# A ring of 21 exponential tiles instead of 14, and another order inside the steps of seven matmul pairs

## The chip, the core and the metric

The kernel runs on one core of a Trainium2 chip. Its engines work in parallel, each through its own queue of instructions in order: TensorE (PE; the loading of its weights is shown as PEld), VectorE (DVE), ScalarE (ACT), GpSimd (POOL), and SyncE (SP), which issues the DMA transfers. They wait for one another through semaphores. The metric is the device time of one execution in microseconds.

## The reference

Attention with one shared key and value head and 32 query heads, a dense layer with Mish, a second dense layer, and a gated residual, on 2048 rows of 512:

```python
xn = _layernorm(x, axis=-1)
# attention: H = 32 heads of Dh = 16, one k and one v for all heads
q = (xn @ wq).reshape(B, S, H, Dh).transpose(0, 2, 1, 3)
k, v = xn @ wk, xn @ wv
p = softmax(einsum("bhqd,bkd->bhqk", q, k) * Dh ** -0.5)
s = einsum("bhqk,bkd->bhqd", p, v).transpose(0, 2, 1, 3).reshape(B, S, H * Dh) @ wo
# dense 512 -> 1792, Mish, dense 1792 -> 512
h = xn @ w1 + b1
g = silu((h * tanh(softplus(h))) @ w2)
return x + s * g
```

## The kernel before

**What a step is.** The 2048 query rows are cut in 4 chunks of 512, the heads in groups of four. A chunk and a group make one of NU = 32 units, and a unit has 16 steps, one for each of the 16 tiles of 128 keys: 512 steps in all. TensorE's 128 rows are used as two lanes of 64 rows, each of which runs its own matmul beside the other's. A step issues on them:

- four scores `e` (line 908), keys by queries. ScalarE turns each into a tile `pt` of exponentials (line 910);
- four matmuls `m` (line 928), the same scores the other way round for a later unit. VectorE takes the maximum of each into `mb` (line 932). From these come the rows that are subtracted before the exponential. Once per unit they are folded and turned (`c_rows`, lines 951 to 961) and moved by DMA;
- up to eight products `xps` of a dense layer (line 112), at three matmuls for each product of 128 (high and low parts). Every product is cut in two halves of 64 rows: one step does the upper halves of a piece, the next the lower halves of the same piece, in the same bank of PSUM;
- last the four `pv` matmuls (line 982) of the exponentials of two steps earlier, which take all 128 rows, and stand in the trace as eight.

**The dense work.** A group of products ends in one 512-wide result. A projection to q, a tile of the first dense layer or of the output layer has 12 products, so two pieces of six and four steps; most thirds of the second dense layer have 15, so pieces of eight and seven. At the end of a group its bank is read out: on ScalarE as `hb` (line 671, first layer), `qf` (611, q) or `y` (739, first third), on VectorE as a sum into `y` (745, and line 156 for the output layer). POOL then splits and multiplies what was read out.

**Banks.** Of the eight banks three are for `e`, three for `m`, one is for `pv` and one for `xps`. Ring `pt` has NPT = 14 tiles of exponentials; the 16 tiles of x first land in the same ring, those beyond its size in two other buffers (`load_x`).

**What sets the order.** Nothing reorders at run time; the program writes each queue out. `waves` (line 537) writes one step. It has a list for the dense lane `h` (`b` and the products `xs`) and one for the other lane (`a`). `em` (line 1339) fills them: the four scores and n of the four maxima go to the other lane in the order of the string EM, the remaining 4 - n maxima to the dense lane, where they are issued after the products. With six or seven products n is 3: the other lane has seven matmuls, the dense lane six or seven products and one m. `waves` takes one of the dense lane and one of the other by turns; such two are called a pair here. The last of the other lane is kept until the products are all issued. What was issued on the other lane when the last product was out is called `relay`: the first product of the next step, in the same bank, is made to wait for ScalarE's or VectorE's instruction of it, unless a group has ended. The lanes change sides from step to step.

The names of this text: T is the first matmul of a step; the first exponential is that of the step's first score; a pair's place is counted from T.

Of the kernel before, what the change touches and what calls it, by code (L numbers as in the profile page):

```python
# [42 lines left out]
HOLD = 1  # L43
STEP_US = 2.95
XMAX = 8
NPT = 14
EM = "MEMEMEME"
MLAG = 4
NHB = 4
NXR = 2  # L50
# [12 lines left out]
def m_need(v):  # L63

    return (34, 64)[v] if v < 2 else 32 * (v + 1)
# [53 lines left out]
def block_kernel(ctx: ExitStack, tc: tile.TileContext, x, wq, wk, wv, wo, w1, b1, w2, out):  # L119
    nc = tc.nc  # L120
# [92 lines left out]
    def load_x(c):  # L213
        for tt in range(4):
            tag, n = ("pt", NPT) if 4 * c + tt < NPT else (("y0", "sc")[tt % 2], 1)
            xin[c, tt] = sb.tile([P, D], F32, tag=tag, name=f"xin{c}_{tt}", bufs=n)
# [252 lines left out]

    held = [None]  # L470
    evacs = [0]
    cur = {"g": None, "ps": None, "n": 0, "chunk": [], "relay": None}

    def is_ready(g):
        return (all(i.tile is not None and i.ready <= step[0] for i in g.items)
# [7 lines left out]
    def begin():  # L483
        prepare()
        if qqueue and is_ready(qqueue[0]):
            g = qqueue.popleft()
        elif queue and is_ready(queue[0]):
            g = queue.popleft()
        else:
            n = next((n for n, g in enumerate(queue) if g.wo is None), None)  # L490
            if not n or not is_ready(queue[n]) or queue[n].m1 is None:
                return False
            g = queue[n]
            del queue[n]
        if g.start:
            g.start()
        if g.alloc:
            ps = g.alloc()
        else:
            ps = ps_x.tile([P, 512], F32, tag="x", name="xps")  # L500
        cur.update(g=g, n=0, ps=ps, chunk=[], relay=None)
        return True

    def finish():
        g = cur["g"]
        if cur["n"] < len(g.mms):
            return False
        for i in g.items:
            i.users -= 1
        cur["g"] = None  # L510
        evacs[0] += g.dve
        if lead:
            lead["post"](g, cur["ps"])
        else:
            g.post(cur["ps"])
            g.done = step[0]
        return True
# [14 lines left out]
    def chunk_size(n):  # L532
        return -(-n // -(-n // XMAX)) if n else 0

    def waves(h, em, new):

        if not cur["chunk"] and (not new or cur["g"] is None and not begin()):  # L540
            mms = []
        else:
            g = cur["g"]
            mms = cur["chunk"] or g.mms[cur["n"]:cur["n"] + chunk_size(len(g.mms) - cur["n"])]
        second = bool(cur["chunk"])
        k = len(mms)
        ms = em(k)
        a = deque(ms[1 - h])
        b = deque(ms[h])
        ps = cur["ps"]  # L550
        ends = second and cur["n"] + k == len(cur["g"].mms)
        xs = deque(mms)
        relay = None
        first = True
        done = False
        while a or b or xs:
            if xs:
                i = xs.popleft().half(ps, h)
                if first and cur["relay"] is not None:
                    tc.add_manual_dep(i.ins, cur["relay"].ins.name, mybir.DependencyInfo(  # L560
                        mybir.DependencyClass.Sync, mybir.DependencyReason.DATA), reason="other half of the bank")
                first = False
                if ends and cur["g"].dve and len(xs) == HOLD:
                    held[0] = []
                if not xs and ends:
                    cur["n"] += k
                    cur["chunk"] = []
                    finish()
                    done = True
                    for top in held[0] or ():  # L570
                        top()
                    held[0] = None
            elif b:
                b.popleft()()
            if len(a) > 1 or a and not xs:
                r = a.popleft()()
                if k and not xs and relay is None:
                    relay = r
        if k and not done:
            assert relay is not None  # L580
            cur["relay"] = relay
            if second:
                cur["n"] += k
                cur["chunk"] = []
            else:
                cur["chunk"] = mms
# [310 lines left out]
    def e_one(s, i):  # L897

        v, r = divmod(s, 16)
        if s < NS - LEAD:  # L900
            a, k, p = 1 - s % 2, r - r % 2 + i // 2, i % 2
        else:
            a, k, p = i % 2, r, i // 2
        q = qt_of[v]
        o = 64 * a
        ps, tag = (ps_m, "m") if NS - LEAD <= s and i in ((1, 3) if s < NS - 4 else (3,)) else (ps_e, "e")
        e = ps.tile([P, C], F32, tag=tag, name=f"e{s}_{i}")
        pe.matmul(e, ks[o:o + 64, P * k:P * (k + 1)], q[o:o + 64, p], start=True, stop=True)  # L908
        pt = sb.tile([P, C], F32, tag="pt", name=f"pt{s}_{i}", bufs=NPT)
        r = act.activation(pt, e, AF.Exp, scale=0.25)  # L910
        pt_of[16 * v + k, p, a] = pt
        return r
# [24 lines left out]
    def m_sides(h, n):  # L937

        ahead = m_next[h] - m_next[1 - h]
        lo = max((4 - MLAG - ahead + 1) // 2, 4 - (32 * NU - m_next[1 - h]))  # L940
        hi = min((4 + MLAG - ahead) // 2, 32 * NU - m_next[h])
        return max(min(n, hi), lo)
# [116 lines left out]
    def due(t):  # L1059
        step[0] = t  # L1060
        for k in sorted(k for k in timed if k <= t):
            for fn in timed.pop(k):
                fn()
# [84 lines left out]
    for c0, c1 in ((0, 1), (1, 2), (2, 3), (3, 4)):  # L1148
# [4 lines left out]
        for c in range(c0, c1):  # L1153
            xs, scs = [], []
# [65 lines left out]
    def best(eng):  # L1220
        found = None
        for k in plan[eng]:
            s = k.start(T[eng])
            if s is not None:
                rank = max(s, T[eng] + 0.1) + WAIT_US * k.prio
                if found is None or rank < found[2]:
                    found = (s, k, rank)
        return found
# [5 lines left out]
    while True:  # L1234
# [7 lines left out]
        b = best("PE")  # L1242
# [13 lines left out]
        s, e, k = min(opts, key=lambda o: o[0])  # L1256
# [34 lines left out]
        elif k == "J":  # L1291
            tag = next((g for g in ("wq", "ws", "wb") if (g == "wq" or s > 19.0) and arrived(g) and busy[0] + E0 < s + 0.5), None)
            n = ran[0]
# [16 lines left out]
    while left:  # L1310
        k = next(k for k in left if all(d.end is not None for d in k.deps))
# [20 lines left out]
    for s in range(NS + 2000):  # L1332
        inm = s < NS - LEAD
        if inm or cur["chunk"]:
            assert s < NS
            due(s)
            h = s % 2

            def em(k):
                n = m_sides(1 - h, k // 2) if inm else 0  # L1340
                x = deque(lambda i=i: e_one(s, i) for i in range(4))
                y = deque(lambda: m_one(1 - h) for _ in range(n))
                r = [[], []]
                for op in EM:
                    if op == "M" and y:
                        r[1 - h].append(y.popleft())
                    elif op == "E":
                        r[1 - h].append(x.popleft())
                r[h] = [lambda: m_one(h) for _ in range(4 - n if inm else 0)]
                return r  # L1350

            if s >= 2 and (s - 1) % 16 == 0 and s > 1:
                gap[0] += 1
            waves(h, em, inm)
            act_jobs(1 + (len(jobs) > 2))
            due(s + 0.5)
            pv_to(s - 2)
            last = s + 1
        elif s < NS:
            if s == last and (NS - s) % 2:  # L1360
                for k in range(4):
                    e_one(s, k)
                due(s)
                fill(4)
                act_jobs(1)
                pv_to(s - 2)
            elif (NS - s) % 2 == 0:
                for k in range(6):
                    e_one(s + k // 4, k % 4)
                due(s)  # L1370
                fill(4)
                act_jobs(1)
            else:
                for k in range(2, 4):
                    e_one(s, k)
                due(s)
                fill(4)
                act_jobs(2)
                pv_to(s - 1)
        else:  # L1380
            due(s)
            act_jobs(100)
            pv_to(NS - 1)
            due(s + 0.5)
            fill(16)
        step[0] = s
        if vdone[0] < 8 * NC and min(m_next) >= m_need(vdone[0]):
            r = c_rows(vdone[0])
            rowq.extend([r[0], lambda r=r: (r[1](), r[2](), r[3]())])
            vdone[0] += 1  # L1390
        if rowq and not evacs[0]:
            rowq.popleft()()
        evacs[0] = 0
        pump()
        if s > NS + 1 and not queue and cur["g"] is None and not timed and not jobs:
            break
# [1 line left out]

# [10 lines left out]
```

## Time and profile before

| | |
|---|---|
| runs, median (lowest to highest) | 1607.55 us (1606.56 to 1608.75) |
| profiled execution, span | 1607.2 us |
| TensorE busy, granted clock | 1590.6 us, 0.996 |
| VectorE, ScalarE, GpSimd busy | 1344.9, 1298.3, 625.4 us |
| start until the first full step | some 93 us |
| regular steps, until some 1530 us | 357 with six products, 60 with seven, 56 with eight |
| end, scores and dense work without maxima | some 77 us |

The span is that of the profiled execution from its first instruction to its last, and is the time against which sums are made. A line of the profile's groups gives engine, operation, tiles, shape and count, then the busy time and the mean of one in ns, then the idle time of the engine before them and who ended it. A line of the timeline gives start and length in us, engine, line and tiles; "x4" are four instructions in a row, and square brackets hold the idle time before them and who ended it. In a table of stretches, each line has the stretch, its length, and for each engine the busy time and the number of instructions, then TensorE's clock and the DMA share.

### The profile page before, as it was taken

How to read it: one execution, taken by the hardware profiler on the slowest of the kernel's cores; microseconds unless marked ns; L12 is line 12 of the kernel's file. 1: busy time of each engine (PE TensorE's matmuls, PEld its weight loads, DVE VectorE, ACT ScalarE, POOL GpSimd, SP SyncE). 2: the span in 40 equal slices, each digit the busy share in tenths (PEclk: the TensorE clock that was granted, in tenths of full speed). 3: DMA queues.
4: the chain of work that ended last, by engine and by line, in shares of the span. 5: the costliest groups of instructions: out<-in, count | busy, mean ns of one | idle time of the engine just before them, and what ended most of it. 6: DMA issues, size and time to landing. Idle time of an engine off the chain costs nothing.

```text
span 1607.2 us, 31497 instructions
## 1 busy us (share of the span) xinstructions
PE 1590.6 (99%) x11611; PEld 847.8 (53%) x11611; DVE 1344.9 (84%) x2299; ACT 1298.3 (81%) x2512; POOL 625.4 (39%) x640
## 2 busy tenths in 40 slices
PE   9999999999999999999999999999999999999998
PEld 5445555555555555555555555555555555555544
DVE  8898888888888888888898988888888888888812
ACT  7478788688898778978988787787798878779885
POOL 3276278066355103612514322172152323315522
PEclk9899999999999999999999999999999999999999
DMA  6233133142321304212103231221331223022020
GB/s 192 72 116 96 51 108 115 29 149 83 101 90 38 111 16 140 64 48 88 39 24 109 64 116 44 87 71 35 96 109 58 83 61 97 24 96 70 8 86 27
DMA packets 73001, 125.08 MB, mean 78 GB/s; under 512 B 21520, under 2 KB 33808, under 8 KB 72848
## 3 DMA queue, kind: packets, MB, share of 16 engines
q1 hardware_dynamic: 72848, 123.08, 24.4%
q8 instruction: 92, 1.51, 0.4%
q14 instruction: 61, 0.50, 0.1%
HBM read 75.57 MB, written 26.21 MB: 63 GB/s over the span
## 4 chain that ended last, share of the span: by engine, by line
PE 96%; DVE 1%; ACT 1%; POOL 0%; DMA 0%; SPq 0%; issue 0%; DVEq 0%; POOLq 0%
PE xps L112 43%; PE pv L982 32%; PE e L908 9%; PE m L928 8%; PE xps L108 3%; PE kp L312 1%; DVE mb L932 1%; PE wop L108 1%; ACT pt L910 0%; PE xp L280 0%; DMA xin<-in_dram 0%; DVE xt L156 0%; SPq L217 0%; ACT hb L671 0%; PE ol L1045 0%
## 5 line engine op out<-in xcount | busy, mean ns | idle before, releaser
L932 DVE TENSOR_REDUCE mb<-m 128x1 f32<-128x512 f32 x2048 | 1271.2, 682 | 184.2 <-PE m L928 149.0
L910 ACT ACTIVATE pt<-e 128x512 f32<-128x512 f32 x2048 | 1068.2, 605 | 250.9 <-PE e L908 240.9
L928 PE MATMUL m<-ks,qt 48*128 48x512 f32 (+1 forms) x2048 | 845.8, 424 | 4.2 <-DVE mb L932 2.9
L908 PE MATMUL e<-qt,ks 64*128 64x512 f32 x2048 | 746.7, 408 | 2.4 <-ACT pt L910 1.6
L982 PE MATMUL pv<-pt,vaug 128*32 128x512 f32 x4096 | 543.1, 604 | 0.0
L928 PEld LDWEIGHTS m<-ks,qt 48*128 48x128 f32 (+1 forms) x2048 | 373.1, 186 | 76.3 <-DVE mb L932 38.0
L908 PEld LDWEIGHTS e<-qt,ks 64*128 64x128 f32 x2048 | 372.4, 186 | 26.2 <-ACT pt L910 11.1
L112 PE MATMUL xps<-xt,ws 64*128 64x512 f32 x1266 | 351.2, 409 | 0.9 <-ACT pt L910 0.4
L112 PEld LDWEIGHTS xps<-xt,ws 64*128 64x128 f32 x1266 | 218.0, 185 | 204.8 <-ACT pt L910 137.7
L112 PE MATMUL xps<-wbs,act 64*128 64x512 f32 x1188 | 321.3, 407 | 0.0
L112 PEld LDWEIGHTS xps<-wbs,act 64*128 64x128 f32 x1188 | 207.0, 185 | 168.7 <-ACT pt L910 103.9
L166 POOL TENSOR_SCALAR t<-t 128x512 f32<-128x512 f32 x56 | 34.4, 614 | 323.8 <-ACT t L679 323.8
L982 PEld LDWEIGHTS pv<-pt,vaug 128*32 128x32 f32 x4096 | 81.9, 108 | 144.1 <-issue 135.8
L156 POOL TENSOR_TENSOR hb<-hb,t 128x512 f32<-128x512 f32 x56 | 72.2, 1289 | 116.1 <-ACT t L692 64.1
L112 PE MATMUL xps<-xt,wq 64*128 64x512 f32 x336 | 93.0, 409 | 0.0
L112 PEld LDWEIGHTS xps<-xt,wq 64*128 64x128 f32 x336 | 57.9, 185 | 54.1 <-ACT pt L910 35.2
L112 PE MATMUL xps<-wbs,ot_all 64*128 64x512 f32 x288 | 79.4, 408 | 0.0
L112 PEld LDWEIGHTS xps<-wbs,ot_all 64*128 64x128 f32 x288 | 49.5, 184 | 46.9 <-ACT pt L910 31.0
L156 POOL TENSOR_TENSOR hb<-hb,u 128x512 f32<-128x512 f32 x56 | 72.2, 1290 | 4.4
L156 POOL TENSOR_TENSOR u<-u,t 128x512 f32<-128x512 f32 x56 | 71.8, 1281 | 4.7
L156 POOL TENSOR_TENSOR act<-hb,act 128x512 fp32r<-128x512 f32 x55 | 70.7, 1286 | 4.6
L156 POOL TENSOR_TENSOR oc<-oc,sc 128x512 f32<-128x512 f32 (+1 forms) x16 | 20.6, 1287 | 121.3 <-ACT sc L1010 110.6
(121 smaller groups left out, 822.4 us busy)
## 6 DMA issues: line engine op xcount, KB each, us to landing
ws<-w SPq DMA_DIRECT2D x38, 512.0 KB
wbs<-w SPq DMA_DIRECT2D x36, 512.0 KB
qt<-qh SPq DMA_DIRECT2D x256, 32.0 KB
wq<-wq SPq DMA_DIRECT2D x14, 512.0 KB
w<-wbs SPq DMA_DIRECT2D x14, 512.0 KB
w<-ws SPq DMA_DIRECT2D x14, 512.0 KB
wbs<-wo SPq DMA_DIRECT2D x12, 512.0 KB
rawwb<-in_dram SPq DMA_DIRECT2D x20, 256.0 KB
```

The lines of the kernel that those rows point to most:

```text
L108: self.pe.matmul(ps, self.lhs(), self.rhs(), start=(self.k == 0), stop=(self.k == self.tot - 1))
L112: i = self.pe.matmul(ps, self.lhs()[o], self.rhs()[o], start=(self.k == 0 and self.halves == 0), stop=(self.k == self.tot - 1 and self.hal ...
L156: eng.tensor_tensor(out=o, in0=a, in1=b, op=op)
L166: pool.tensor_scalar(o, o, lim, 0.0, op0=ALU.min, op1=ALU.max)
L312: pe.matmul(kp_of[c], wkf[:, dt], xf_of[c][dt // 2][:, dt % 2], start=(dt == 0), stop=(dt == 3))
L908: pe.matmul(e, ks[o:o + 64, P * k:P * (k + 1)], q[o:o + 64, p], start=True, stop=True)
L910: r = act.activation(pt, e, AF.Exp, scale=0.25)
L928: pe.matmul(m, q[o, p, P * t:P * (t + 1)], ks[o, C * kb:C * (kb + 1)], start=True, stop=True)
L932: return dve.reduce_max(out=mb_of[v][:, kb, z:z + 1], in_=m, axis=AX.X)
L982: pe.matmul(o[32 * j:32 * j + 32], vaug[:, k], pt, start=(k == 0), stop=(k == 15))
```

## The change

NPT goes from 14 to 21. The string that orders the other lane becomes a table: with three maxima on it the order is e m e m e e m, with four it is as before. `waves` gets a mark, `front`: in a step where the other lane has seven matmuls, the dense lane's maximum is issued first, ahead of the products. The program's scratch area for descriptors that software makes is set to 1024 bytes; the larger ring takes its room.

```diff
-NPT = 14
-EM = "MEMEMEME"
+NPT = 21
+ORDERS = {3: "EMEMEEM", 4: "MEMEMEME"}
...
-    cur = {"g": None, "ps": None, "n": 0, "chunk": [], "relay": None}
+    cur = {"g": None, "ps": None, "n": 0, "chunk": [], "relay": None, "front": False}
...
         ms = em(k)
+        cur["front"] = k > 0 and len(ms[1 - h]) == 7
...
         while a or b or xs:
-            if xs:
+            if xs and b and first and cur["front"]:
+                b.popleft()()
+                cur["front"] = False
+            elif xs:
...
-                for op in EM:
+                for op in ORDERS.get(n, "MEMEMEME"):
...
-    nc = bacc.Bacc("TRN2", target_bir_lowering=False, num_devices=1)
+    nc = bacc.Bacc("TRN2", target_bir_lowering=False, num_devices=1,
+                   dynamic_dma_scratch_size=1024)
```

On TensorE, the first six matmuls of one step of six products, in the middle of a group, before and then now (`m` maxima, `e` scores, `xps` products; the wait in brackets names the engine whose count it waits for):

```order
L112 MATMUL xps<-xt_9025,ws_12528 128x512 [waits Activation_49]
L928 MATMUL m_1_1_12796<-ks,qt_77 128x512 [waits DVE_49]
L112 MATMUL xps<-xt_9025,ws_12528 128x512
L908 MATMUL e_0_12800<-qt_78,ks 128x512
L112 MATMUL xps<-xt_9025,ws_12528 128x512
L928 MATMUL m_1_2_12805<-ks,qt_77 128x512 [waits DVE_49]
```

```order
L932 MATMUL m_0_31_12795<-ks,qt_79 128x512 [waits DVE_49]
L912 MATMUL e_0_12798<-qt_78,ks 128x512 [waits Activation_49]
L112 MATMUL xps<-xt_9025,ws_12528 128x512 [waits DVE_49]
L932 MATMUL m_1_1_12803<-ks,qt_77 128x512
L112 MATMUL xps<-xt_9025,ws_12528 128x512
L912 MATMUL e_1_12807<-qt_78,ks 128x512 [waits Activation_49]
```

The first score has moved from the second pair to the first, the first product from the first pair to the second, and the product's wait is for VectorE instead of ScalarE.

The end of the same step on TensorE, from the fourth product or so to the first `pv`, before and then now:

```order
L112 MATMUL xps<-xt_9025,ws_12528 128x512
L928 MATMUL m_1_3_12814<-ks,qt_77 128x512 [waits DVE_49]
L112 MATMUL xps<-xt_9025,ws_12528 128x512
L908 MATMUL e_2_12818<-qt_78,ks 128x512 [waits Activation_49]
L928 MATMUL m_0_31_12822<-ks,qt_79 128x512 [waits DVE_49]
L908 MATMUL e_3_12825<-qt_78,ks 128x512 [waits Activation_49]
L982 MATMUL pv_12395<-pt_0_12756,vaug 32x512
```

```order
L112 MATMUL xps<-xt_9025,ws_12528 128x512
L912 MATMUL e_2_12816<-qt_78,ks 128x512 [waits Activation_49]
L112 MATMUL xps<-xt_9025,ws_12528 128x512
L912 MATMUL e_3_12821<-qt_78,ks 128x512 [waits Activation_49]
L112 MATMUL xps<-xt_9025,ws_12528 128x512
L932 MATMUL m_1_3_12826<-ks,qt_77 128x512 [waits DVE_49]
L986 MATMUL pv_12395<-pt_0_12755,vaug 32x512
```

The fourth score stands in the sixth pair instead of the seventh; the last product and a maximum stand last.

On ScalarE, the end of a group of the first dense layer and the step behind it, before and then now (`hb` is the read-out):

```order
L910 ACTIVATE pt_0_12672<-e_0_12670 128x512 [waits PE_49]
L910 ACTIVATE pt_1_12681<-e_1_12679 128x512 [waits PE_49]
L671 ACTIVATE hb_3_12688<-xps,b1c 128x512 [waits PE_49]
L910 ACTIVATE pt_2_12692<-e_2_12690 128x512 [waits PE_49]
L910 ACTIVATE pt_3_12699<-e_3_12697 128x512 [waits PE_49]
L910 ACTIVATE pt_0_12717<-e_0_12715 128x512 [waits PE_49,Activation_49]
```

```order
L914 ACTIVATE pt_0_12670<-e_0_12668 128x512 [waits PE_49]
L914 ACTIVATE pt_1_12679<-e_1_12677 128x512 [waits PE_49]
L914 ACTIVATE pt_2_12688<-e_2_12686 128x512 [waits PE_49]
L914 ACTIVATE pt_3_12693<-e_3_12691 128x512 [waits PE_49]
L675 ACTIVATE hb_3_12696<-xps,b1c 128x512 [waits PE_49]
L914 ACTIVATE pt_0_12715<-e_0_12713 128x512 [waits PE_49]
```

The read-out has moved behind the fourth exponential, and the next step's first exponential no longer waits for ScalarE's own count beside TensorE's.

## The prediction

> **What bounds the kernel.** I read the page first, then the stretches of long runs of equal steps, then two single steps instruction by instruction.
>
> ```profile
> PE 1590.6 (99%) x11611; PEld 847.8 (53%) x11611; DVE 1344.9 (84%) x2299; ACT 1298.3 (81%) x2512; POOL 625.4 (39%) x640
> PEclk9899999999999999999999999999999999999999
> q1 hardware_dynamic: 72848, 123.08, 24.4%
> ```
>
> TensorE is busy 99% at the full clock. But two matmuls run side by side in the two halves of its rows, so a lane that is held for a tenth of a microsecond does not show as idle: busy time hides the losses. They have to be read from the length of a step. The stretches below list, for the pv matmuls alone, length and count; a step has 8 of them.
>
> ```profile
> 318.50:550.10 231.60, 85.23 (x640) 12.61 (x640) 1.00 0.30 94
> 784.84:958.38 173.54, 63.94 (x480) 9.45 (x480) 1.00 0.24 72
> 1190.35:1364.62 174.27, 63.93 (x480) 9.45 (x480) 1.00 0.24 76
> 958.38:1007.72 49.34, 17.05 (x128) 2.52 (x128) 1.00 0.18 56
> ```
>
> The first three are runs of steps with six dense products, 80+60+60 = 200 steps in 579.41 us: **2.897 us a step**. The fourth has 16 steps of seven or eight: 3.084. By the order of the program 357 of the 500 steps are of the six-product kind, 60 have seven and 56 eight, so 357 x 2.897 = 1034 us hang on the first kind.
>
> Two such steps, with TensorE's first matmul, first and last score e, and first pv of each:
>
> ```profile
> 799.33 0.50 PE L112 MATMUL xps<-wbs,act 64*128 64x512 f32 x1
> ...
> 799.68 0.39 PE L908 MATMUL e<-qt,ks 64*128 64x512 f32 x1
> ...
> 800.83 0.43 PE L908 MATMUL e<-qt,ks 64*128 64x512 f32 x1
> ...
> 801.18 1.07 PE L982 MATMUL pv<-pt,vaug 128*32 128x512 f32 x8
> 802.18 0.50 PE L112 MATMUL xps<-wbs,act 64*128 64x512 f32 x1
> ...
> 802.52 0.40 PE L908 MATMUL e<-qt,ks 64*128 64x512 f32 x1
> ...
> 803.68 0.49 PE L908 MATMUL e<-qt,ks 64*128 64x512 f32 x1
> ...
> 804.10 1.07 PE L982 MATMUL pv<-pt,vaug 128*32 128x512 f32 x8
> 805.09 0.50 PE L112 MATMUL xps<-wbs,act 64*128 64x512 f32 x1
> ```
>
> They last 2.85 and 2.91. What a step of eight pairs without a hold looks like (first matmul, last pair, pv, next step):
>
> ```profile
> 1527.31 0.50 PE L112 MATMUL xps<-wbs,act 64*128 64x512 f32 x1
> ...
> 1529.05 0.39 PE L928 MATMUL m<-ks,qt 48*128 48x512 f32 x1
> 1529.36 1.07 PE L982 MATMUL pv<-pt,vaug 128*32 128x512 f32 x8
> 1530.36 1.17 PE L908 MATMUL e<-qt,ks 64*128 64x512 f32 x6
> ```
>
> 3.05 us: pv 0.31 behind the last pair, and 1.00 more. Seven pairs without a hold are one pair (0.23) less, 2.82. So the two steps above are held 0.03 and 0.09. The holder is the fourth score's weights:
>
> ```profile
> 800.11 2.07 ACT L910 ACTIVATE pt<-e 128x512 f32<-128x512 f32 x4 [0.28 <-PE e L908]
> 803.01 2.06 ACT L910 ACTIVATE pt<-e 128x512 f32<-128x512 f32 x4 [0.33 <-PE e L908]
> ...
> 800.76 0.18 PEld L908 LDWEIGHTS e<-qt,ks 64*128 64x128 f32 x1
> 803.67 0.18 PEld L908 LDWEIGHTS e<-qt,ks 64*128 64x128 f32 x1
> ```
>
> There are three banks for scores, so the fourth waits for the first exponential to be read out. In the first step that exponential starts 0.43 after its matmul, ends at 800.71 (0.60 long), and the weights go out 0.05 later; pv follows 0.42 after them. In the second it starts 0.49 after its matmul: by the order of the program this one waits for two counts, TensorE's and ScalarE's own (the tile of the ring that it overwrites), and the extra 0.06 goes straight into the step. 236 of the 512 first exponentials of a step wait for two.
>
> **The change, part by part.** Times are counted from the step's first matmul; how many places are of a kind is counted in the order of the two programs.
>
> *Ring of 21.* In the changed program 1 of the 512 first exponentials waits for two counts; 73 second ones do, and they queue behind the first anyway (four exponentials in 2.07, so 0.48 apart). That 0.06 is gone. Tiles 14 and 15 of x land in the ring instead of two other buffers: same transfers, no cost. The smaller scratch area belongs to software-made descriptors; every data packet above is on q1, so nothing is taken from it. TensorE's weights still wait on three banks, which the ring does not add to.
>
> *Order, ordinary step.* The first score now stands in the first pair, the fourth in the sixth. A first-pair score is seen in a step that has no dense product:
>
> ```profile
> 98.71 0.49 PE L908 MATMUL e<-qt,ks 64*128 64x512 f32 x1
> ...
> 99.27 2.06 ACT L910 ACTIVATE pt<-e 128x512 f32<-128x512 f32 x4
> ```
>
> The exponential starts 0.56 later, since the first matmul behind pv is longer. It ends at 1.16, the fourth score's weights go out at 1.21, one pair follows (0.23), then pv: 1.21 + 0.42 + 0.23 = 1.86, and the step is 2.86. The new order thus holds as long as the old one.
>
> *The hand-over between the halves.* The first dense product of a step waits for what was issued last on the other lane of the step before. That was the third (or fourth) exponential; now it is the fourth maximum on VectorE, in 339 places against 42 before.
>
> ```profile
> 802.75 2.48 DVE L932 TENSOR_REDUCE mb<-m 128x1 f32<-128x512 f32 x4 [0.36 <-PE xps L112]
> ```
>
> The four maxima end 3.05 into their step (805.23 - 802.18), which is 0.19 into the next; with 0.05 for the signal the weights go out at 0.24, and the matmul 0.11 later (0.42 from weights to pv less 0.31 from pair to pv), at 0.35. It is due at 0.34, since it stands in the second pair. So VectorE just covers it, with nothing to spare; m and e behind it on TensorE are issued in order. An ordinary step costs 2.86, and 357 x (2.897 - 2.86) = **-13.2 us**.
>
> *Group ends, ScalarE.* The bank of the dense products is single; the next group's first product waits until it is emptied. The last product moves from the sixth pair to the seventh, and the read-out on ScalarE from between the second and third exponential to behind the fourth.
>
> ```profile
> L671 ACT ACTIVATE hb<-xps,b1c 128x512 f32<-128x512 f32 x56 | 38.7, 691 | 9.1 <-PE xps L108 9.1
> L739 ACT ACTIVATE y<-xps 128x512 f32<-128x512 f32 x16 | 9.8, 613 | 0.0
> L611 ACT ACTIVATE qf<-xps 128x512 f32<-128x512 f32 x15 | 9.1, 605 | 5.5 <-PE xps L108 5.5
> ```
>
> Fourth exponential at 0.56 + 3 x 0.48 = 2.00, hb at 2.48, done 3.17, weights 3.22, matmul 3.33: 0.47 into the next step, due 0.34. Less the 0.04 by which that step is held anyway, 0.09; 43 such ends are followed by a six-product step: +3.9. Where an eight-product step follows, a dense product is in the first pair and its weights are due at 0: 0.36 x 6 (hb) + 0.28 x 4 (qf) = +3.3. Behind y (a step of 3.05): 2.48 + 0.61 + 0.05 - 3.05 = 0.09 x 10 = +0.9.
>
> *Group ends, VectorE.* The sum y is added from the same bank. Shown is a seven-product step before: its start, y, and the next step's weights, held until y is done.
>
> ```profile
> 682.94 0.50 PE L112 MATMUL xps<-wbs,act 64*128 64x512 f32 x1
> ...
> 685.31 0.68 DVE L745 TENSOR_TENSOR y<-xps,y 128x512 f32<-128x512 f32 x1
> ...
> 686.05 0.18 PEld L112 LDWEIGHTS xps<-wbs,act 64*128 64x128 f32 x1 [0.90 <-DVE y L745]
> ```
>
> y goes in at 2.37, ends 3.05. In six-product steps it now lies there too, and the fourth maximum ends at 3.65. The third m of the next step, now in pair four (0.80), wants its bank: 3.65 + 0.05 + 0.11 - 2.86 = 0.95. Late by 0.15, less 0.04: 0.11 x 24 = +2.6.
>
> *Row maxima of a head.* Every 16 steps the maxima of a head are folded and turned:
>
> ```profile
> 784.97 0.16 DVE L954 TENSOR_REDUCE mp<-mp 128x16 fp32r<-128x16 f32 x1
> ...
> 785.56 0.21 DVE L961 STREAM_TRANSPOSE cr<-mp 128x32 f32<-128x32 f32 x1 [0.22 <-DVE mp L956]
> 785.70 1.84 DVE L932 TENSOR_REDUCE mb<-m 128x1 f32<-128x512 f32 x3
> ```
>
> VectorE is 0.73 late, free at 2.97 + 0.73 = 3.70 or 0.84 into the next step, where the first maximum is due at 0.57. The fourth m then waits for the first maximum's bank (0.84 + 0.68 + 0.16 = 1.68 against 1.50; 0.12 to 0.14 net), as now; new is that the next step's dense product waits for the late fourth maximum too: 0.13. 0.25 x 26 = +6.5.
>
> *pv's read-out*, at the end of each head:
>
> ```profile
> 796.45 0.50 PE L112 MATMUL xps<-wbs,act 64*128 64x512 f32 x1
> ...
> 796.59 0.60 ACT L991 ACTIVATE os<-pv 128x512 f32<-128x512 f32 x1 [0.15 <-PE pv L982]
> ```
>
> It starts at 0.14; the first exponential follows 0.48 later, at 0.62 instead of 0.56: 0.06 x 22 = +1.3. Before, the first score came late enough not to meet it.
>
> Seven-product steps have eight pairs either way and their fourth score holds nothing: 0.
>
> Sum: -13.2 + 3.9 + 3.3 + 0.9 + 2.6 + 6.5 + 1.3 = **+5.3** on the profiled execution's span of 1607.2. The median of the runs, 1607.55, is 0.35 above it: 1612.9, said as **1613**.
>
> Bounds: if the first-pair exponential came 0.54 after its matmul (0.44 as in the second pair, plus 0.10 of longer matmul), the step would be 2.84 and the sum 7 lower. I take the measured 0.56. If the two limits, score bank and hand-over, add up instead of covering each other, a step gains nothing: +13. The group and head terms (18.5 together) can be nothing or half as much again.
>
> **A rule on bubbles.** The same hold returns in every seven-pair step in front of pv. The Trainium skill, Perfetto Trace Analysis, "Optimization Strategy", says that a gap which repeats on the engine that should be full can mean too little SBUF or PSUM for the next tile. Here the trace gives both a part: 0.06 in some steps to the ring in SBUF, 0.03 to the score banks, to which nothing is added. What the sum would be if the ring alone were short stands as the second rival.
>
> **Rivals.** *Group ends are covered (faster).* If the evacuations ended by 3.04 instead of 3.17, the next product's weights would go out in time, and the 10.7 us of group ends fall away: 1602; if the head terms fell too, 1595. For it: today they are covered.
>
> ```profile
> PEld xps L112 <- ACT pt L910: 307.8, 368, 0.8
> ...
> PEld xps L112 <- ACT hb L671: 31.0, 37, 0.8
> ```
>
> Weight loads pause 0.84 (307.8/368) during pv whoever releases them, and behind hb the pause is no longer (31.0/37). Against: the order puts the read-out behind all four exponentials. *The hold vanishes with the ring.* Then VectorE's hand-over is the limit, 2.85 a step, 357 x 0.047 = 16.8 less: with the terms above 1609, no measurable change. Against: the trace shows the hold in steps with one count too. *The hand-over holds every step (much slower).* If VectorE's fourth maximum ends 0.05 to 0.1 later than in the old order, each of some 270 hand-overs pays it: 1627 to 1640. Against: m stands early enough, VectorE idles 0.36 before each first maximum. *Only the ring acts*: 236 x 357/512 = 165 steps by 0.06, 9.9 us: 1598; it needs the order to cost nothing, and counts with the first.
>
> **Numbers.** Forecast 0.47 (1611 to 1624), much slower 0.08, cancelling 0.19, covered group ends or ring alone 0.26. A measurement of this kernel can tell about 0.2%, 3.2 us: faster 0.26, same 0.19, slower 0.55. Range 1600 to 1625, which leaves out the ends of the first and third rival.
>
> **What would show it.** Right: first exponentials 0.56 after their matmul in all six-product steps, no mode at 2.91, steps near 2.86; the wait of xps weights on maxima large where it was absent, steps behind hb 0.1 longer, behind a head's fold 0.1 to 0.2. Wrong: xps weights never late behind hb, or ordinary steps at 2.82 or above 2.90.

## The result

The changed kernel takes 1615.33 us, median of 5 runs (1613.0 to 1619.4), against 1607.55 (1604.81 to 1608.75, five runs; the table further up has the first three of them) before: a ratio of 1.0051 with a 95% interval of 1.0036 to 1.0066. It is slower by half a per cent, 7.8 us; forecast were 1613 and slower.

### The profile page after: what moved, and what is told of

The parts are those of the page before. It is cut to its first block, busy times and chain, and to the rows that moved or that the text cites. A ratio compares the mean times of both kernels' runs of the same rounds, so it can differ in the third digit from the quotient of the medians.

```text
span 1611.2 us, 31203 instructions
## 1 busy us (share of the span) xinstructions
PE 1591.2 (99%) x11611; PEld 845.3 (52%) x11611; DVE 1343.8 (83%) x2299; ACT 1302.8 (81%) x2512; POOL 625.2 (39%) x640
## 4 chain that ended last, share of the span: by engine, by line
PE 93%; ACT 3%; DVE 3%; issue 0%; DMA 0%; POOL 0%; SPq 0%; DVEq 0%; ACTq 0%; POOLq 0%
PE xps L112 34%; PE pv L986 30%; PE m L932 17%; PE e L912 7%; ACT pt L914 2%; DVE mb L936 2%; PE xps L108 2%; PE kp L312 1%; PE wop L108 1%; PE xp L280 0%; ACT y L743 0%; DMA xin<-in_dram 0%; DVE xt L156 0%; ACT hb L675 0%; ACT qf L615 0%
## 5 line engine op out<-in xcount | busy, mean ns | idle before, releaser
L932 PE MATMUL m<-ks,qt 48*128 48x512 f32 (+1 forms) x2048 | 793.9, 427 | 3.8 <-DVE mb L936 2.4
L912 PE MATMUL e<-qt,ks 64*128 64x512 f32 x2048 | 779.8, 425 | 2.5 <-ACT pt L914 1.5
L932 PEld LDWEIGHTS m<-ks,qt 48*128 48x128 f32 (+1 forms) x2048 | 363.8, 185 | 390.9 <-DVE mb L936 372.6
L112 PE MATMUL xps<-xt,ws 64*128 64x512 f32 x1266 | 334.1, 396 | 0.6 <-POOL ws L156 0.4
L112 PE MATMUL xps<-wbs,act 64*128 64x512 f32 x1188 | 310.7, 398 | 2.4 <-ACT hb L675 1.0
L112 PEld LDWEIGHTS xps<-wbs,act 64*128 64x128 f32 x1188 | 213.1, 185 | 80.3 <-ACT pt L914 21.8
L112 PEld LDWEIGHTS xps<-xt,ws 64*128 64x128 f32 x1266 | 226.4, 185 | 33.8 <-ACT hb L675 4.7
L112 PE MATMUL xps<-xt,wq 64*128 64x512 f32 x336 | 88.4, 396 | 0.0
L112 PE MATMUL xps<-wbs,ot_all 64*128 64x512 f32 x288 | 75.2, 394 | 0.0
L749 DVE TENSOR_TENSOR y<-xps,y 128x512 f32<-128x512 f32 x32 | 21.9, 683 | 51.2 <-PE xps L108 51.2
```

The source lines that it names most:

```text
L112: i = self.pe.matmul(ps, self.lhs()[o], self.rhs()[o], start=(self.k == 0 and self.halves == 0), stop=(self.k == self.tot - 1 and self.hal ...
L749: dve.tensor_tensor(out=y, in0=ps, in1=y, op=ALU.add)
L932: pe.matmul(m, q[o, p, P * t:P * (t + 1)], ks[o, C * kb:C * (kb + 1)], start=True, stop=True)
```

## The profile after

The first lines of the page say as little as before: TensorE is busy 99%.

```profile
PE 1591.2 (99%) x11611; PEld 845.3 (52%) x11611; DVE 1343.8 (83%) x2299; ACT 1302.8 (81%) x2512; POOL 625.2 (39%) x640
PEclk9999999999999999999999999999999999999999
```

The stretches answer more. These are the same four runs of steps as before, for the pv matmuls alone (stretch, length, busy time and count on TensorE and its weight loads, clock, DMA share, GB/s):

```profile
316.01:548.78 232.77, 85.23 (x640) 12.60 (x640) 1.00 0.30 93
784.46:958.60 174.14, 63.92 (x480) 9.45 (x480) 1.00 0.24 71
1191.42:1366.23 174.81, 63.92 (x480) 9.45 (x480) 1.00 0.25 76
958.60:1008.42 49.82, 17.05 (x128) 2.52 (x128) 1.00 0.18 53
```

581.72 / 200 = 2.909 us for a step of six products (2.897 before), 49.82 / 16 = 3.114 for one of seven or eight (3.084 before). Over the whole run, with a step measured from its first matmul to the next step's, the 360 six-product steps (the prediction counted 357) take 1049.8 us instead of 1042.2, the sevens 185.8 instead of 185.0, the eights 185.6 instead of 185.3 (60 of each): 8.7 us more in all.

The profiled execution's span is 1611.2, only 4.0 more than before. The rest lies in the start, where the two executions had different clocks. All engines in the first 80 us (TensorE, its weight loads, VectorE, ScalarE, GpSimd, then clock, DMA share and GB/s), after:

```profile
0.00:80.00 80.00, 73.26 (x291) 40.83 (x292) 71.38 (x149) 46.53 (x104) 31.14 (x42) 1.00 0.42 133
```

and before:

```profile
0.00:80.00 80.00, 74.20 (x270) 41.14 (x271) 68.34 (x141) 45.55 (x102) 26.39 (x37) 0.91 0.41 133
```

At a granted clock of 1.00 TensorE got through 291 matmuls in that stretch, at 0.91 through 270, and the first full step began at 88.67 instead of 93.15. The ten kernels profiled below began it at 88 to 98 us, eight of them at clocks of 0.94 to 0.96. The rings of 21 and of 16, both with the order of before and both at 0.94, began it at 92.9 and 93.1. So the 4.5 us by which the start is shorter are put down to the clock and not to the change, and the steps are compared.

**An ordinary step.** Two in a row, on TensorE (first score, fourth score, pv, first matmul of the next step), ScalarE and the weight loads:

```profile
799.05 0.50 PE L912 MATMUL e<-qt,ks 64*128 64x512 f32 x1
799.62 2.06 ACT L914 ACTIVATE pt<-e 128x512 f32<-128x512 f32 x4 [0.30 <-PE e L912]
...
800.27 0.18 PEld L912 LDWEIGHTS e<-qt,ks 64*128 64x128 f32 x1
800.93 1.06 PE L986 MATMUL pv<-pt,vaug 128*32 128x512 f32 x8
801.93 0.50 PE L932 MATMUL m<-ks,qt 48*128 48x512 f32 x1
...
802.50 2.07 ACT L914 ACTIVATE pt<-e 128x512 f32<-128x512 f32 x4 [0.30 <-PE e L912]
803.15 0.18 PEld L912 LDWEIGHTS e<-qt,ks 64*128 64x128 f32 x1
803.82 1.07 PE L986 MATMUL pv<-pt,vaug 128*32 128x512 f32 x8
804.81 0.50 PE L932 MATMUL m<-ks,qt 48*128 48x512 f32 x1
```

Both last 2.88. The first exponential starts 0.57 after its matmul (799.62 - 799.05), the fourth score's weights go out at 1.22, pv follows 0.66 to 0.67 later, the next step 1.00 after that. Before, such steps came in two kinds, near 2.85 and near 2.91: of the 360, 126 were under 2.858 and 181 over 2.895. Now none is under 2.858, 233 lie between, and 127 are over 2.895. The short kind has gone with the long one.

**Waits.** Weight loads, by what they waited for (total us, times, longest):

```profile
PEld m L932 <- DVE mb L936: 372.6, 460, 0.8
PEld xps L112 <- ACT pt L914: 23.2, 28, 0.8
...
PEld xps L112 <- ACT hb L675: 9.5, 38, 1.2
```

The pause of the weight loads during pv, 0.81 in the mean, is now put down to the maximum in front and no longer to the dense product. That is also why the total behind hb has fallen, from 31.0 to 9.5; the longest wait there has grown from 0.8 to 1.2.

**Behind a read-out on ScalarE.** One group end, with the step behind it (its first matmul is at 946.89):

```profile
944.59 2.06 ACT L914 ACTIVATE pt<-e 128x512 f32<-128x512 f32 x4 [0.82 <-PE m L932]
946.51 0.71 ACT L675 ACTIVATE hb<-xps,b1c 128x512 f32<-128x512 f32 x1
946.89 0.50 PE L932 MATMUL m<-ks,qt 48*128 48x512 f32 x1
...
947.27 0.18 PEld L112 LDWEIGHTS xps<-xt,ws 64*128 64x128 f32 x1 [0.20 <-ACT hb L675]
947.28 0.49 PE L112 MATMUL xps<-xt,ws 64*128 64x512 f32 x1
...
947.61 0.40 PE L112 MATMUL xps<-xt,ws 64*128 64x512 f32 x1
...
948.88 1.06 PE L986 MATMUL pv<-pt,vaug 128*32 128x512 f32 x8
949.88 0.50 PE L932 MATMUL m<-ks,qt 48*128 48x512 f32 x1
```

hb ends at 947.22, the product's weights go out 0.05 later, at 0.38 of the step; the first product also runs longer (0.33 to the next instead of 0.23). pv starts at 1.99, and the step lasts 2.99.

## The experiments

Where an experiment says "order of before", its edit holds the two lines of the first one. Three groups of kernels were each timed beside the kernel before on one chip; its median was 1607.04 (26 runs) beside the ring, the order, the ring of 16 and the earlier read-out, 1609.51 (13) beside the three on the limits of the step and the fold in three steps, 1606.77 (12) beside the two last kernels.

### The ring alone

```diff
 NPT = 21
-ORDERS = {3: "EMEMEEM", 4: "MEMEMEME"}
+ORDERS = {}
...
-        cur["front"] = k > 0 and len(ms[1 - h]) == 7
+        cur["front"] = False
```

> Ring of 21, order of before. In the program the first exponentials that wait for two counts fall from 236 to 1. Theory: the ring is worth only that wait, 0.06 us in some 165 steps of six products, 9.9 us: 1597.6 us, steps of six products at 2.85 with no group at 2.91. Rival (the ring is worth nothing, TensorE was not held by it): 1607.5 us, as before. Rival (a larger ring is worth more than the wait): below 1592 us.

Measured: 1601.05 us (1599.2 to 1605.61), ratio 0.9951 (0.9932 to 0.9971). The ring makes the kernel half a per cent faster. The six-product runs, pv alone:

```profile
317.51:547.37 229.86, 85.23 (x640) 12.59 (x640) 1.00 0.30 95
780.68:952.90 172.22, 63.92 (x480) 9.44 (x480) 1.00 0.23 72
1183.93:1356.30 172.37, 63.93 (x480) 9.44 (x480) 1.00 0.25 77
```

574.45 / 200 = 2.872. The 360 steps take 1033.6, 8.6 less than before, and 247 of them are under 2.858. This is the step that lasted 2.91 in the prediction's rows:

```profile
798.01 0.50 PE L112 MATMUL xps<-wbs,act 64*128 64x512 f32 x1
...
798.35 0.40 PE L912 MATMUL e<-qt,ks 64*128 64x512 f32 x1
...
798.79 2.06 ACT L914 ACTIVATE pt<-e 128x512 f32<-128x512 f32 x4 [0.26 <-PE e L912]
...
799.86 1.07 PE L986 MATMUL pv<-pt,vaug 128*32 128x512 f32 x8
800.85 0.49 PE L112 MATMUL xps<-wbs,act 64*128 64x512 f32 x1
```

Its first exponential starts 0.44 after its matmul instead of 0.49, and it lasts 2.84. The trace of before bears this out step by step: in 162 of the 360 six-product steps the first exponential waits for two counts, and all 162 last over 2.895 (median 2.912); the 126 under 2.858 are all among the other 198 (median 2.851). The exponential starts 0.495 after its matmul in the first kind and 0.436 in the second. So the second count was worth 0.06 in the step.

### The order alone

```diff
-NPT = 21
+NPT = 14
```

> Ring of 14, new order in steps of seven pairs. In the program 34 first exponentials wait for two counts (236 before, 1 in the changed kernel): the new order alone moves most of the second waits to the third exponential. Theory: the waits are all that the ring does, so 34 x 357/512 x 0.06 = 1.4 us over the changed kernel, about 1617 us. Rival (ring and order are independent parts, the ring 9.9 us whatever the order): 1625 us.

Measured: 1615.92 us (1614.19 to 1621.93), ratio 1.0051 (1.0034 to 1.0069): the same as with 21 tiles. First of the three runs of steps, pv alone:

```profile
319.00:551.81 232.81, 85.24 (x640) 12.59 (x640) 1.00 0.30 93
```

232.77 with 21 tiles, 232.81 with 14. By the order of the two programs the ring of 14 leaves only 34 of the 512 first exponentials with two counts in the new order (236 in the old), and by the trace none of them in a six-product step; 121 third ones have two, and those queue behind two others. The order thus takes away the very cost that the ring was to remove, and the ring has nothing left to give. The order's own price is the distance of the changed kernel to the ring alone: 1049.8 - 1033.6 = 16.2 us of steps. The medians of ring alone and order alone, timed together, are 14.9 apart.

### A ring of 16

The order of before, and

```diff
-NPT = 21
+NPT = 16
```

> Order of before, ring of 16. In the program 236 first exponentials wait for two counts, just as with 14. Theory: the count of these waits decides, not the room: 1607.5 us, as before. Rival (room in the ring decides): between 1598 and 1605 us.

Measured: 1607.35 us (1605.08 to 1613.69), ratio 0.9993 (0.9978 to 1.0008). Second run of steps, pv alone:

```profile
784.81:958.42 173.61, 63.92 (x480) 9.44 (x480) 1.00 0.23 72
```

173.61 against 173.54 before and 172.22 with 21. Two tiles more change nothing as long as 236 first exponentials wait for two counts; 162 of the six-product steps are again among them, and all 162 last over 2.895. It is the second wait that costs, not the room in the ring. This kernel also has the smaller scratch area of the changed one, which thus costs nothing either.

### What holds the ordinary step: half of every maximum

```diff
-            return dve.reduce_max(out=mb_of[v][:, kb, z:z + 1], in_=m, axis=AX.X)
+            return dve.reduce_max(out=mb_of[v][:, kb, z:z + 1], in_=m[:, 0:C // 2], axis=AX.X)
...
-        r = act.activation(pt, e, AF.Exp, scale=0.25)
+        r = act.activation(pt, e, AF.Exp, scale=0.02)
```

> The changed kernel, but each maximum is taken over half of its 512 columns, and the exponentials are scaled by 0.02 instead of 0.25 so that they stay finite: the softmax is another one, TensorE, ScalarE and every wait stay. VectorE's maxima shorten to about 0.35 us, so the hand-over between the halves, the y on VectorE and the fold of a head can no longer hold TensorE. Theory (the score banks hold an ordinary step): steps stay at 2.87 to 2.88; only the steps behind a fold and behind y shorten, 5 us: 1610 us. Rival (the hand-over from the fourth maximum holds it): 2.82 a step, 357 x 0.06 = 21 us more: 1589 us.

Measured: 1605.5 us (1603.9 to 1609.17), ratio 0.9976 (0.9967 to 0.9986). VectorE's group of maxima, in the changed kernel and here, and the second run of steps:

```profile
L936 DVE TENSOR_REDUCE mb<-m 128x1 f32<-128x512 f32 x2048 | 1271.7, 683 | 188.8 <-PE e L912 113.4 <-PE m L932 70.4 <-PE xps L112 4.2
L936 DVE TENSOR_REDUCE mb<-m 128x1 f32<-128x256 f32 x2048 | 819.2, 422 | 617.0 <-PE e L912 362.9 <-PE m L932 211.3 <-PE xps L112 31.7
```

```profile
783.25:956.70 173.45, 63.92 (x480) 9.44 (x480) 1.00 0.23 71
```

VectorE works some 452 us less on maxima and idles 617 us ahead of them instead of 189, and yet the median ordinary step is 2.877, as in the changed kernel. Had the hand-over through the fourth maximum held it, it would have become shorter. The 360 steps gain 2.9 us in all, and they gain them where VectorE is late: steps with a fold go from 2.952 to 2.872, those behind a sum y or an output tile on VectorE from 2.92 to 2.88. Those behind hb stay at 3.02. The medians lie further apart, by some 12 us (ratios 0.9976 and 1.0051), and a good part of that is the granted clock: in this group the kernel before ran at 0.993 to 0.999 and the half maxima at 0.997 to 1.000. At 0.998 the kernel before took 1607.1, the half maxima 1606.9 to 1607.3 and the changed kernel, in its own group, 1614.1. So the half maxima are not told apart from the kernel before, and about 7 us separate them from the changed kernel: 2.9 in the six-product steps, 1.4 in the sevens and eights, the rest open.

### The fourth score one pair later

```diff
-ORDERS = {3: "EMEMEEM", 4: "MEMEMEME"}
+ORDERS = {3: "EMEMEME", 4: "MEMEMEME"}
```

> The changed kernel with the other lane e m e m e m e: the fourth score back in the seventh pair, the fourth maximum in the sixth. Theory (three banks each, the fourth waits for the first to be read): the first maximum ends 1.26 into the step, the weights of the fourth m go out at 1.31, pv follows 0.42 + 0.23 later, a step of six products is 2.95 to 2.97; 357 x 0.08 = 28 us over the changed kernel: 1643 us. Rival (only the score banks hold a step, the fourth score in the seventh pair is free): 2.82 a step, 357 x 0.06 = 21 us less: 1594 us.

Measured: 1634.79 us (1634.07 to 1639.5), ratio 1.0156 (1.0139 to 1.0173); the median step is 2.937, a little less than expected. One step, on TensorE, VectorE and the weight loads:

```profile
820.29 0.50 PE L932 MATMUL m<-ks,qt 48*128 48x512 f32 x1
...
820.83 2.48 DVE L936 TENSOR_REDUCE mb<-m 128x1 f32<-128x512 f32 x4 [0.46 <-PE e L912]
...
821.57 0.18 PEld L932 LDWEIGHTS m<-ks,qt 48*128 48x128 f32 x1
...
822.24 1.06 PE L986 MATMUL pv<-pt,vaug 128*32 128x512 f32 x8
823.23 0.49 PE L932 MATMUL m<-ks,qt 48*128 48x512 f32 x1
```

The step's fourth maximum is now in the sixth pair, and its weights go out at 1.28: the first maximum starts on VectorE at 0.54 and is 0.68 long, so its bank is read at 1.22. The score bank no longer holds, since the score behind it comes later than the bank is free; in its place the bank of the maxima does, and longer, since a maximum takes 0.68 and an exponential 0.60.

### Both limits out of the way

```diff
-ORDERS = {3: "EMEMEEM", 4: "MEMEMEME"}
+ORDERS = {3: "EMEMEME", 4: "MEMEMEME"}
```

with the half maxima of the experiment before the last.

> The same half maxima and scale with the other lane e m e m e m e. Theory: with the fourth score in the seventh pair (due 1.39, free at 1.21) and the short maxima both banks are free in time and nothing holds an ordinary step: 2.82, 357 x 0.06 = 21 us less than with half maxima alone: about 1589 us, and less again where the read-out of the bank now stands ahead of the fourth exponential (7 us): 1582. Rival (something else holds the step, such as the products or the switch to pv): as with half maxima alone, 1610 us.

Measured: 1578.72 us (1575.13 to 1579.12), ratio 0.9804 (0.9788 to 0.9821). One step and a run of steps:

```profile
785.23 0.49 PE L932 MATMUL m<-ks,qt 48*128 48x512 f32 x1
...
785.76 1.62 DVE L936 TENSOR_REDUCE mb<-m 128x1 f32<-128x256 f32 x4 [1.20 <-PE e L912]
...
787.05 1.07 PE L986 MATMUL pv<-pt,vaug 128*32 128x512 f32 x8
788.05 0.49 PE L932 MATMUL m<-ks,qt 48*128 48x512 f32 x1
```

```profile
768.06:938.08 170.02, 63.93 (x480) 9.44 (x480) 1.00 0.24 73
```

The step is 2.82 (median of all 360: 2.824), the value that the prediction had derived for seven pairs without a hold. With the maxima halved, moving the fourth score back by one pair takes 0.05 off each step. The same move changes the hand-over to the dense lane: in the program 293 of the 360 six-product steps of the changed kernel wait there for VectorE, and 314 of this one for ScalarE, as in the kernel before. That is no rival, since the first product of an ordinary step stands at 0.34 (median) in the changed kernel, with half maxima alone, with the later score alone and with both, which is where it is due. Together the three settle that in the changed kernel the score bank holds the ordinary step.

### The read-out ahead of the fourth exponential

At the end of a group of twelve products that is read out on ScalarE, the fourth exponential is issued after the read-out:

```diff
+                if ends and not cur["g"].dve and len(xs) == HOLD and k == 6:
+                    late[0] = []
...
                     held[0] = None
+                    for bottom in late[0] or ():
+                        bottom()
+                    late[0] = None
...
-        r = act.activation(pt, e, AF.Exp, scale=0.25)
         pt_of[16 * v + k, p, a] = pt
-        return r
+
+        def bottom():
+            return act.activation(pt, e, AF.Exp, scale=0.25)
+        if late[0] is None:
+            return bottom()
+        late[0].append(bottom)
```

> The changed kernel, but at the end of a group of twelve the fourth exponential is issued on ScalarE behind the read-out of the bank instead of ahead of it; TensorE's and VectorE's queues are unchanged. Theory: the 0.09 (43 times), 0.36 (6) and 0.28 us (4) behind group ends are the read-out's lateness and go away, 7 us: 1608 us, and no step behind an hb above 2.90. Rival (the steps behind group ends are long for another reason, such as VectorE): 1615 us.

Measured: 1609.63 us (1607.05 to 1612.9), ratio 1.0005 (0.9992 to 1.0019), not to be told from the kernel before. ScalarE at the group end shown above:

```profile
945.16 1.58 ACT L923 ACTIVATE pt<-e 128x512 f32<-128x512 f32 x3 [0.80 <-PE e L918]
946.61 0.70 ACT L681 ACTIVATE hb<-xps,b1c 128x512 f32<-128x512 f32 x1
947.18 0.62 ACT L923 ACTIVATE pt<-e 128x512 f32<-128x512 f32 x1
948.04 2.08 ACT L923 ACTIVATE pt<-e 128x512 f32<-128x512 f32 x4 [0.24 <-PE e L918]
```

Steps behind hb fall from 3.012 to 2.893, and the 360 steps by 6.7 us to 1043.1. So the ends of groups on ScalarE make up most (6.7 of 8.7 us) of what the changed kernel loses against the one before.

### The fold of the row maxima, spread out

Two ways to spread VectorE's work of a fold, on the changed kernel. In three steps:

```diff
-            rowq.extend([r[0], lambda r=r: (r[1](), r[2](), r[3]())])
+            rowq.extend([r[0], r[1], lambda r=r: (r[2](), r[3]())])
```

> The changed kernel with the fold of a head's maxima spread over three steps instead of two (the second and third reduction a step apart), so that no step has over 0.4 us of it on VectorE, which idles 0.4 before each first maximum; the rows are moved a step later. Theory: the step with the fold (now 0.03 over the others) and the step behind it (0.15) become ordinary, 26 x 0.18 = 4.7 us: 1610.5 us. Rival (these steps are long for another reason, or the later rows are waited for): 1615 us or more.

Measured: 1666.41 us (1665.19 to 1670.77), ratio 1.0359 (1.034 to 1.0378), a miss. TensorE's waits:

```profile
PE e L912 <- DMA qt<-cr: 31.5, 23, 3.8
```

and the same wait in the changed kernel:

```profile
PE e L912 <- DMA qt<-cr: 1.0, 1, 1.0
```

The steps with a fold became ordinary ones (median 2.88), as meant. But the rows that the fold yields go by DMA into the q tiles of the next head, and that head's first scores now waited for them 23 times, up to 3.8 us. In the changed kernel this wait stood once, for 1.0, and in the kernel before once, for 0.8. The rows had been arriving just in time: with their transfers issued one step later, the kernel takes some 50 us more than the changed one. In the trace the first steps of the heads are 50.3 us longer together, all other steps 1.0. In two even steps, with the DMA where it was:

```diff
-            rowq.extend([r[0], lambda r=r: (r[1](), r[2](), r[3]())])
+            rowq.extend([lambda r=r: (r[0](), r[1]()), lambda r=r: (r[2](), r[3]())])
```

> The changed kernel with the fold of a head in two steps as before, but its second reduction is done in the first step: 0.25 + 0.35 us of VectorE there and only the turn in the second, so the rows move no later than in the changed kernel. Theory (a late first maximum makes the fold's step and the one behind it long): the first maximum is 0.13 late instead of 0.27, the fourth m is no longer held and the hand-over 0.1: 26 x 0.1 = 2 to 3 us less, 1613 us, with the steps behind a fold at 2.98 at most. Rival (what made the fold over three steps slow was the fold and not the later rows): 1616 us or more, with steps over 4 us at the start of a head.

Measured: 1614.34 us (1610.87 to 1619.93), ratio 1.0044 (1.0024 to 1.0063). Steps with a fold fall from 2.952 to 2.890, those behind them stay at 2.96; 1.0 us of steps in all, less than the runs tell from nothing.

### The best of it

The ring of 21, the order of before, and the even fold:

> Ring of 21, order of before, and the same even fold. Theory: with only the ring, steps of a fold last 2.975 and the others 2.85; with the even fold the fourth m is held at most 0.02, so 26 x 0.1 = 2.7 us less than with the ring alone: 1598.4 us. Rival (the fold's steps are long for another reason): 1601 us.

Measured: 1597.5 us (1595.03 to 1603.58), ratio 0.9945 (0.9924 to 0.9966). Two of the three runs of steps:

```profile
315.66:544.66 229.00, 85.22 (x640) 12.59 (x640) 1.00 0.31 95
777.14:949.45 172.31, 63.92 (x480) 9.44 (x480) 1.00 0.24 72
```

It is faster than both kernels of this case. Against the ring alone (0.9951) it is not told apart: its 360 steps take 1032.4 instead of 1033.6.

## Why the prediction was right, and where it was not

The sign, the size (+5.3 forecast, 8.7 in the steps, 7.8 in the medians) and the mechanism hold: the ordinary step gained little, and the ends of groups and heads cost more than that. Term by term, with the measured side as count times the excess over the changed kernel's median ordinary step, 2.877:

| term | predicted, us | measured, us |
|---|---|---|
| ordinary step, against 2.897 | -13.2 (2.86) | -7.1 (357 x 0.020) |
| behind hb, six-product step | +3.9 | +5.8 (43 x 0.135) |
| behind qf, six-product step | 0 | +0.4 (9 x 0.045) |
| ScalarE ends ahead of an eight-product step | +3.3 | +2.7 (6 x 0.30 + 4 x 0.23) |
| behind y, seven to eight | +0.9 | +1.4 (10 x 0.14) |
| behind sums on VectorE | +2.6 | +1.3 (17 x 0.04 + 12 x 0.055) |
| fold and the step behind it | +6.5 | +2.8 (22 x 0.075 + 13 x 0.09) |
| pv's read-out | +1.3 | +0.9 (16 x 0.054) |
| sum | +5.3 | +8.2 |

The two rows ahead of an eight-product step are measured as the growth of the pair of steps against before. That the sum came this near is partly chance: the terms that came out above the forecast are 8.9 us off together, those that came out below it 6.0, and the two offset each other.

- *Ordinary step: right in kind, mis-sized by 0.02.* "First exponential 0.56 after e, weights at 1.21, pv at 1.86" measured 0.57, 1.22 and 1.88 to 1.89; that the score bank is the limit was shown by halving the maxima with and without the later fourth score. The 0.02 are the largest error of the sum, 6.1 us. They are hundredths in each link: the exponential starts at 0.565 in the median, and pv follows the weights by 0.66 instead of 0.65. The 0.42 from weights to pv was read in the first of the prediction's two steps; the second has 0.43 (804.10 - 803.67), and so has the median ordinary step with the ring alone.
- *The hand-over just covers: right.* The first product of an ordinary step stands at 0.34, where it was due, and the step did not shrink when VectorE was given 0.26 less work per maximum. What should show it did not: the wait of the dense product's weights on maxima is not large (3.8 us in 10 places), since a maximum now leads TensorE's queue and the pause of pv is booked there.
- *Ends on ScalarE: right in place and too small.* Weights were predicted at 0.36 of the step behind hb, and went out at 0.38. The step came out at 2.99 in the median (mean 3.01), not 2.95. What was mis-sized is the lateness of the dense lane: the product was put 0.13 late; it came 0.05 late, but the next pair followed after 0.33 instead of 0.23, and the sixth product stands at 1.65 instead of 1.50. pv is 0.11 late (1.99 against 1.88), so "less the 0.04 by which that step is held anyway" held. The mean is 0.135, in part because in nine of the 43 steps the product waits for two counts, ScalarE's and GpSimd's: its weights go out 0.11 to 0.12 after hb's end there instead of 0.05, and the steps last 3.02 to 3.08. Issuing the read-out one exponential earlier gave 6.7 us back, which shows the cause.
- *Ends on VectorE and the fold: right in sign, about half as large.* Halving the maxima took most of both away (2.92 to 2.88 behind a sum, 2.952 to 2.872 in a fold's step, 2.965 to 2.89 behind it), so they do come from VectorE; the chain of waits that was set up for each was too pessimistic, and which link of it had slack stays open. That a fold delays the step behind it is new with the order, as forecast: 2.852 there with the ring alone, 2.965 with the changed order.
- *Ring: right in mechanism, wrong in what it is worth here.* The ring alone was put at 9.9 us and gave 8.6. In the sum it had no term of its own, but the part on the ring says that its 0.06 "is gone" by the ring. It is gone by the order: with 14 tiles the changed order takes the same time.
- *Rivals.* Covered group ends: no, the wait behind hb grew to 1.2. The hold vanishes with the ring: no; 2.82 came only with half maxima and another place for the fourth score. The hand-over holds every step: no, the ordinary step is 2.877. The Trainium skill (Perfetto Trace Analysis, "Optimization Strategy") says that a gap repeated on the engine that should be full can mean too little SBUF or PSUM for the next tile. The runs bear out the part on PSUM, and of SBUF only that 16 tiles give nothing and 21 give half a per cent, by the count of waits. Only the ring acts: that is the kernel with the ring alone, and it would have needed the order of before.

## What to carry to other kernels

Before an instruction that waits is moved, its new place should be checked against every bank and every hand-over of the step: here scores, maxima and the dense bank were each within 0.1 us of being the limit. When two edits come together, build each alone before adding their gains, for here both removed the same wait, and one of them had a price. And price the rare places (group ends, folds, heads) beside the ordinary step: 2.88 against 2.897 looked like a gain, and some hundred longer steps more than took it back.

## What was not expected of the hardware

- A second wait on an engine's own count costs ScalarE 0.06 us when it is idle (0.495 against 0.436 from matmul to exponential, medians of 162 and 198 steps). On TensorE a second wait showed the same: in nine steps of the changed kernel that follow hb, the weights went out 0.11 to 0.12 after its end with it, and 0.05 without. Behind a queue of other exponentials it costs nothing that the times show: the changed order with 14 tiles, where such waits sit on queued exponentials, takes as long as with 21, where they are few.
- The same 80 us at the start ran at a granted clock from 0.89 to 1.00 in the twelve executions profiled, and the first full step began at 88 to 98 us, latest at the lowest clock. Over whole runs it is alike: of the 26 runs of the kernel before in the first group, those at 1.000 took 1603.8 to 1606.0 us, the two at 0.993 took 1612.3 and 1613.2. A span alone, or a few runs at other clocks, can hide or feign a change of half a per cent.
- A transfer of a few rows that showed one wait of 1.0 us in all cost some 50 us when issued one step later.
